# Window attention and a feed-forward net on one core: joining a pair's transposes to the next scores in one step of TensorE, with four PSUM banks for attention and a new order

## The chip, the cores and the metric

The kernel runs on one core of one Trainium2 chip. The metric is the device time of one execution in microseconds (us), taken as the median of several runs. A core has five engines that run side by side: TensorE (PE in the profile; its weight loads are a row of their own, PEld), VectorE (DVE), ScalarE (ACT), GpSimd (POOL) and SyncE (SP), which issues the DMAs. Only TensorE multiplies matrices. It writes into PSUM, eight banks of 128 partitions x 512 float32, and DVE and ACT read the banks out again.

## The reference, cut to what matters

Eight batches, eight heads, 512 local and 32 global positions, head dimension 64; then a feed-forward net on 4352 tokens of 512 features with 2048 hidden ones.

```
s_g   = scale * q_g @ k_all.T            # 32 global queries see all 544 keys
out_g = sm(s_g) @ v_all
s_ll  = where(|i - j| <= 32, scale * q_l @ k_l.T, -1e9)    # 512 local queries: a window
s_lg  = scale * q_l @ k_g.T                                # and the 32 global keys
out_l = sm(concat(s_lg, s_ll)) @ concat(v_g, v_l)
x     = attention's output, heads side by side: (4352, 512)
h     = x @ w_in;  out = (h - tanh(h)) @ w_out
```

## The kernel before, in words

**Attention.** Heads go in pairs (class `Pair`), 32 of them, four to a batch; a pair's two heads sit on the two halves of the 128 partitions. A pair has four tiles of 128 local queries, taken in two halves (`tp` 0 and 1, two tiles each). A half goes through these steps:

- *Scores* (`add_head_scores`, L588): keys of a window of 192 and the 32 globals against 128 queries, 64 rows of the array at a time. Two PSUM banks, one for each head. From the third batch on ("split" pairs, 24 of them) keys and queries are each a rounded high part and a rest, and three products are added: 12 matmuls. In the first two batches they are plain float32, which the profile shows as 8.
- *Softmax* (`Head.add_softmax`, `add_norms`): the maximum with the mask, from the banks into `prob` (DVE, L866); the exponential (ACT, L873); the inverse of the sum (DVE, L603 and L604); the scaling (POOL, L610).
- *Transposes* (`add_transposes`, L631): 16 small matmuls turn the probabilities, again 64 rows at a time, into two banks, one for each half of the rows; two copies bring them to `keys_first` (DVE or ACT, L309).
- *Product* (`add_product`, L655): the turned probabilities with the values, 64 columns of the array at a time, into one bank; then DVE and ACT write it as the high part and the rest of x (`x_hi`, `x_lo`, L309 and L666).

The global queries of a pair have steps of their own (L515 and L516 in the first two batches, L747 and L748 after), with softmax and a transpose (on TensorE in the first two batches, L555; on DVE after, L790). The first two batches also turn keys and queries on TensorE (L482).

**Feed-forward.** A batch of 512 rows makes a `Chunk` of 16 steps. *Hidden* (`add_hidden`, L936): three parts of four matmuls, 128 rows x 128 columns of the array with 512 moving columns, into one bank; tanh on ACT (L944), a subtraction on DVE (L947) that frees the bank, then the high part (`ghi`) and the rest (`glo`, POOL L953). *Out* (`add_out`, L984): three parts of four matmuls, one for each 128 rows, into four banks that are kept for the whole chunk. The weights come as 64-bit numbers and are taken apart on chip while the first batches' attention runs.

**Who decides the order.** The kernel writes nothing down by hand. Each step is given to `Order.add` with the engines that can do it, a cost, a due time, what it reads and writes and the PSUM banks that it takes (`alloc`) and gives back (`free`). `Order.run` then plays the whole program through once while the kernel is built: it picks again and again the step that can start first, the due time deciding among those that start within `TOL` of each other, and calls the steps' functions in the order of the starts. Each engine then runs its instructions in that order. The due times are offsets of the table `CFG`. TensorE's steps have a mode: "f" (the whole array, feed-forward), "r" (64 rows: scores and transposes) and "c" (64 columns: products); the player adds `SWITCH` where it changes.

**Banks.** Banks 4 to 7 are the out steps' sums. Banks 0 to 3 are for hidden steps ("h"); attention from the second batch on ("att") may use 0, 1 and 2 of them. In the first batch it may use all eight.

**Names.** `prob` has one buffer for each head and tile parity from the second batch on, so a half's softmax can't start to write before the other half's transposes have read. The split keys and queries (`kw`, `hl`, `hi`, `wraw`), the raw loads (`rawkq`) and the values have one buffer each.

Of the kernel before, what the change touches and what calls it, by code (L numbers as in the profile page):

```python
# [16 lines left out]
P = 128  # L17
# [28 lines left out]
class Op:  # L46
    __slots__ = ("eng", "fn", "due", "n", "ready", "succ", "alloc", "free", "lat", "start", "end", "args", "seq", "xfer", "rows", "ldw", "tail", "lock", "mode")


class Order:  # L50
# [14 lines left out]
    def add(self, eng, fn, due, r=(), w=(), res=(), alloc=(), free=(), lat=0.0, xfer=0.0, rows=1.0, ldw=0.107, tail=0.107, lock=False, mode="f"):  # L65
        o = Op()
# [19 lines left out]
        for k in w:  # L86
            self.writer[k] = o
            self.readers[k] = []
        self.ops.append(o)
# [17 lines left out]
    def run(self):  # L107
# [8 lines left out]
        out = []  # L116
        while left:
            best = None
            for o in ready:
# [26 lines left out]
            ready.remove(o)  # L146
            left -= 1
# [36 lines left out]
def kernel(ctx, tc, q_l, k_l, v_l, q_g, k_g, v_g, w_in, w_out, out):  # L184
# [89 lines left out]
    def bank(shape, j, dt=F32):  # L274
# [6 lines left out]
        elif len(shape) == 4:  # L281
# [4 lines left out]
    CFG = dict(a_g=0.1528, a_kg=0.2722, a_ph=0.3445, a_qs=0.5857, a_w=0.1978, a_wn=0.303, a_xg=0.0853, d_g=28.2389, d_gl=1.4069,  # L286
               d_kg=0.574, d_kq=0.0553, d_ph=0.7721, d_pl=0.4774, d_qh=0.1505, d_qs=0.7921, d_tg=914.3225, d_tp=0.5309,
               d_w=61.785, d_wl=29.9535, d_wn=2.2777, d_xg=0.8447, d_y=0.1584, gfirst=0, ho=18.3348, hs=7.7357, lag=58.6742,
               last=24.9751, o_st0=69.8962, o_st1=113.8499, o_tw0=-1431.7355, o_tw1=129.7041, one=0, p0=160.4863, pen=3.9779,
               penp=0.8319, s_g=0.3958, s_gl=0.5029, s_kq=0.6844, s_p=0.1545, s_tg=40.9569, s_w=0.5334, s_wl=0.6576,  # L290
               step=38.5209, step1=-59.4443, lag0=99.5779, hs0=26.4451, tol=0.0037, xs=0.0037, xw=2.0259, o_ld0=-383.5097,
               o_tn0=1414.0372, o_sg0=1109.3583, o_tg0=75.7936, o_s0=247.2865, o_sp0=242.3207, o_t0=1074.9507, o_tpp0=394.0123,
               o_vl0=1388.0707, o_vl1=952.0056, o_pv0=1892.5728, o_pvp0=670.2065, o_ld1=347.8113, o_pv1=573.0431,
               o_pvp1=217.9889, o_s1=-211.9116, o_sg1=-321.0909, o_sp1=169.903, o_t1=-1979.8578, o_tg1=442.9271, o_tn1=464.4544,
               o_tpp1=-937.5482, ho0=79.3549, o_tg=2112.2434, o_pv=263.2194, o_pvp=714.503, o_s=-1629.8233, o_sp=859.0595,
               o_t=-381.019, o_tpp=-111.4941, o_tn=-1300.494, o_ld=40.8961, o_lq=274.0963, o_sg=-2095.3744, o_st=-628.0791,
               o_tw=-371.5237, o_vl=-1824.1943, o_gl=170.0508, a_kw=0.0458, d_kw=0.5405, s_kw=0.8377, wdi=19.213, wdo=0.1788)
# [4 lines left out]
    order = Order({"att": (0, 1, 2), "h": (0, 1, 2, 3), "acc": (4, 5, 6, 7), None: tuple(range(8))})  # L302
# [141 lines left out]
    class Pair:  # L444
# [126 lines left out]
        def add_head_scores(self, tp):  # L571
# [3 lines left out]
            def mm(e, tags):  # L575
# [14 lines left out]
            due = self.due(self.C["o_s"] + self.C["o_sp"] * tp)  # L590
            reads = ["kw0", "kl0", "kg0", "hk0", "lq"] if split else self.key[2:]
            add(("T", 0.76 if split else 0.85), mm, due, r=reads, w=names, res=[a.p(tp) for a in self.heads],
                alloc=[(n, self.tag) for n in names], rows=0.8 if split else 1.0, tail=0.093 if split else 0.187, mode="r")
            for a in self.heads:
                a.add_softmax(tp)
            self.add_norms(tp)

# [19 lines left out]

        def add_transposes(self, tp):
            names = [(f"t{tp}{x}", self.j) for x in range(2)]
            box = {}  # L620

            def mm(e, tags):
                for x in range(2):
                    box[x] = bank([P, 2, 4, 64], tags[names[x]])
                for h, a in enumerate(self.heads):
                    for i in range(2):
                        src = a.pt(2 * tp + i)
                        for c in range(2):
                            for x in range(2):
                                r = slice(64 * x, 64 * x + 64)  # L630
                                nc.tensor.transpose(box[x][:, h, 2 * c + i], src[r, c * P:(c + 1) * P], idn[r, r])  # L631

            def store(x):
                def fn(e, _):
                    copy(e, view(keys_first[:, 0, tp], [(2 * 768, 2), (192, 4), (1, 64)], 64 * x), box[x])
                return fn

            due = self.due(self.C["o_t"] + self.C["o_tpp"] * tp)
            add(("T", 0.55), mm, due, r=[a.p(tp) for a in self.heads] + ["idr"], w=names, res=[f"h{tp}0", f"h{tp}1"], alloc=[(n, self.tag) for n in names],
                rows=0.7, ldw=0.053, tail=0.053, mode="r")  # L640
            for x in range(2):
                add(either(512, "tp", True), store(x), due + 0.5, r=[names[x]], w=[f"h{tp}{x}"], free=[(names[x], 1)])
# [264 lines left out]
    class Chunk:  # L907
# [8 lines left out]
        def add_hidden(self, s):  # L916
# [52 lines left out]
        def add_out(self, s):  # L969
# [22 lines left out]
            if last:  # L992
                for tt in range(nt):
                    g = [(tt, f, wi, gi, f - fs[0]) for f in fs for wi, gi in passes]
                    add(("T", 0.2305 * len(g)), mm(g), due + 0.1 * tt, r=[gk, lk] + wk, w=[accs[tt], ("ord", self.name)])
            else:
                for i, (wi, gi) in enumerate(passes):
                    g = [(tt, f, wi, gi, f - fs[0]) for f in fs for tt in range(nt)]
                    add(("T", 0.2305 * len(g)), mm(g), due + 0.1 * i, r=[(gk, lk)[gi]] + wk, w=accs,
# [87 lines left out]
    def attention(j):  # L1087
        p, split = pairs[j], j >= H
        if split:
            p.add_keys()  # L1090
            p.add_split_global_scores()
        else:
            p.add_turn()
            p.add_global_scores()
            if j + 1 == H // 2:
                add_first_globals(1)
            if j + 2 < H // 2:
                pairs[j + 2].add_load()
            elif H // 2 <= j + 1 < H:
                pairs[j + 1].add_load()  # L1100
        for a in p.heads:
            a.add_values()
        if split:
            for h in range(2):
                p.add_split_global_transpose(h)
        else:
            p.add_global_transpose()
        for tp in range(2):
            p.add_head_scores(tp)
            if tp and H <= j + 1 < len(pairs):  # L1110
                if (j + 1) % (H // 2) == 0:
                    add_globals(pairs[j + 1].b)
                pairs[j + 1].add_split()
            p.add_transposes(tp)
# [100 lines left out]
```

## Time and profile before

| | before |
|---|---|
| median of 3 runs | 1007.95 us (1007.91 to 1008.49) |
| the profiled execution: time, span | 1008.14 us, 1006.4 us |
| busy: PE, PEld | 985.8, 786.5 us |
| busy: DVE, ACT, POOL | 467.2, 520.6, 447.9 us |
| PE waits after 110 us | none |
| first feed-forward matmul | at 60.03 us |

All durations come from one profiled execution. Its time is 1.7 us more than its span, which runs from the first instruction to the last, and 0.19 us more than the median of the runs. The timeline lists runs of equal instructions with the start of the first, the time from there to the end of the last, and their count. Ends of matmuls are modelled and overlap; what one costs is read from start to start.

### The profile page before, as it was taken

Reading aid. Unit: us, or ns where it says so; the run is one execution under the profiler, and the core shown is the slowest. Engines: PE = TensorE matmul, PEld = TensorE weight load, DVE = VectorE, ACT = ScalarE, POOL = GpSimd, SP = SyncE. Lnnn points to the kernel's source line nnn. Section 1 sums busy time; section 2 is a strip of 40 time slices with the busy share of each in tenths; the row PEclk is TensorE's granted clock in tenths of the full one; section 3 lists DMA queues with packets and bytes.
Section 4 is the critical chain, followed back from the end, with each engine's and each line's share of the span. In section 5 each row is a group of like instructions: output and inputs, shape, how many; then the busy total and the mean of one; then the engine's idle time right before and its main releaser. Section 6 shows DMA issues by size and latency. Waiting matters only on the chain.

```text
span 1006.4 us, 18022 instructions
## 1 busy us (share of the span) xinstructions
PE 985.8 (98%) x6352; PEld 786.5 (78%) x6352; DVE 467.2 (46%) x1532; ACT 520.6 (52%) x1444; POOL 447.9 (45%) x575
## 2 busy tenths in 40 slices
PE   7799999999999999999999999999999999999997
PEld 5567777787777778877877787778787788888896
DVE  6986556644445554444544444544444442111110
ACT  6877666555545555555545454655555453322221
POOL 4676756544435454445443444344534342322221
PEclk9889999999999999999999999999999999999999
DMA  8666333321222221321212121321222200100010
GB/s 216 175 193 182 99 78 93 82 45 29 42 56 67 40 43 29 77 40 34 52 29 77 36 36 31 79 44 25 51 39 72 40 2 19 42 1 1 1 42 22
DMA packets 203130, 59.36 MB, mean 59 GB/s; under 512 B 187936, under 2 KB 196128, under 8 KB 203040
## 3 DMA queue, kind: packets, MB, share of 16 engines
q1 hardware_dynamic: 203040, 58.21, 24.4%
q8 instruction: 50, 0.82, 0.3%
q14 instruction: 40, 0.33, 0.1%
HBM read 49.27 MB, written 8.91 MB: 58 GB/s over the span
## 4 chain that ended last, share of the span: by engine, by line
PE 95%; DVE 2%; SPq 1%; ACT 1%; DMA 1%; issue 0%; DVEq 0%
PE bank L936 38%; PE bank L984 38%; PE bank L655 7%; PE bank L588 5%; PE bank L631 4%; PE bank L747 1%; PE bank L748 0%; DMA first_q<-in_moe_w_in_dram 0%; PE bank L482 0%; DVE keys_first L309 0%; SPq L466 0%; DVE st L603 0%; PE bank L515 0%; DVE prob L866 0%; DMA first_raw<-in_k_l_dram 0%
## 5 line engine op out<-in xcount | busy, mean ns | idle before, releaser
L953 POOL TENSOR_TENSOR glo<-t,ghi 128x512 fp32r<-128x512 f32 x136 | 175.9, 1293 | 358.8 <-ACT ghi L309 218.0
L947 DVE TENSOR_TENSOR t<-bank,t 128x512 f32<-128x512 f32 x136 | 94.0, 691 | 237.3 <-ACT t L944 236.7
L944 ACT ACTIVATE t<-bank 128x512 f32<-128x512 f32 x136 | 81.5, 599 | 172.5 <-PE bank L936 168.8
L610 POOL TENSOR_SCALAR prob<-prob,st 128x224 f32<-128x224 f32 x240 | 107.1, 466 | 108.2 <-DVE st L604 100.6
L984 PE MATMUL bank<-w_out_hi,glo 128*128 128x512 f32 x544 | 153.4, 396 | 0.0
L984 PE MATMUL bank<-w_out_hi,ghi 128*128 128x512 f32 x544 | 152.6, 394 | 0.0
L984 PE MATMUL bank<-w_out_lo,ghi 128*128 128x512 f32 x544 | 151.2, 392 | 0.0
L873 ACT ACTIVATE prob<-prob,st 128x224 f32<-128x224 f32 x240 | 112.8, 472 | 59.0 <-DVE st L866 58.9
L936 PE MATMUL bank<-x_lo,w_in_hi 128*128 128x512 f32 x512 | 142.0, 399 | 0.0
L936 PE MATMUL bank<-x_hi,w_in_lo 128*128 128x512 f32 x512 | 140.3, 396 | 0.0
L936 PE MATMUL bank<-x_hi,w_in_hi 128*128 128x512 f32 x512 | 138.5, 392 | 1.3 <-DVE x_hi L309 1.3
L866 DVE CUSTOM_DVE_ANT_0 prob<-bank,mask 128x224 f32<-128x224 f32 x240 | 79.8, 387 | 95.1 <-PE bank L588 93.9
L984 PEld LDWEIGHTS bank<-w_out_hi,glo 128*128 128x128 f32 x544 | 99.8, 188 | 24.1 <-issue 4.2
L984 PEld LDWEIGHTS bank<-w_out_hi,ghi 128*128 128x128 f32 x544 | 100.6, 188 | 22.9 <-issue 1.6
L984 PEld LDWEIGHTS bank<-w_out_lo,ghi 128*128 128x128 f32 x544 | 101.2, 188 | 21.6 <-issue 0.7
L309 ACT CAST ghi<-t 128x512 fp32r<-128x512 f32 x136 | 84.7, 622 | 54.7 <-DVE t L947 45.5
L936 PEld LDWEIGHTS bank<-x_hi,w_in_hi 128*128 128x128 f32 x512 | 94.4, 188 | 22.3 <-ACT keys_first L309 1.7
L936 PEld LDWEIGHTS bank<-x_hi,w_in_lo 128*128 128x128 f32 x512 | 93.7, 188 | 22.8 <-issue 4.0
L936 PEld LDWEIGHTS bank<-x_lo,w_in_hi 128*128 128x128 f32 x512 | 92.8, 188 | 22.4 <-issue 0.6
L309 ACT COPY keys_first<-bank 128x512 f32<-128x512 f32 (+2 forms) x126 | 56.6, 496 | 78.2 <-PE bank L631 77.2
L655 PE MATMUL bank<-keys_first,values 128*64 128x160 f32 (+2 forms) x1024 | 82.3, 302 | 3.8 <-DVE keys_first L309 3.3
L655 PEld LDWEIGHTS bank<-keys_first,values 128*64 128x64 f32 (+1 forms) x1024 | 64.1, 139 | 11.6 <-DVE keys_first L309 3.9
(144 smaller groups left out, 1174.7 us busy)
## 6 DMA issues: line engine op xcount, KB each, us to landing
out_dram<-wpair SPq DMA_DIRECT2D x32, 256.0 KB, 2.0
values<-in_v_l_dram SPq DMA_DIRECT2D x63, 128.0 KB, 2.3
rawkq<-in_k_l_dram SPq DMA_DIRECT2D x96, 64.0 KB, 2.3
rawkq<-in_q_l_dram SPq DMA_DIRECT2D x96, 64.0 KB, 2.2
values<-in_v_l_dram SPq DMA_DIRECT2D x63, 64.0 KB, 2.5
stage<-in_moe_w_out_dram SPq DMA_DIRECT2D x6, 512.0 KB, 4.1
first_q<-in_moe_w_in_dram SPq DMA_DIRECT2D x6, 512.0 KB, 4.2
wpair<-in_moe_w_out_dram SPq DMA_DIRECT2D x6, 512.0 KB, 4.1
```

The costliest lines, as they stand in the source:

```text
L309: (nc.scalar.copy if e == "A" else nc.vector.tensor_copy)(dst, src)
L588: nc.tensor.matmul(x[:, i, :KC], q, k, start=n == 0, stop=n == len(passes) - 1)
L610: nc.gpsimd.tensor_scalar(x, x, st[:, c:c + 1], 1.0, op0=ALU.mult, op1=ALU.mult)
L631: nc.tensor.transpose(box[x][:, h, 2 * c + i], src[r, c * P:(c + 1) * P], idn[r, r])
L655: nc.tensor.matmul(box["o"][h.e:h.e + D, o0:o0 + c1 - c0], values[:k, h.two, a, t], keys_first[:k, h.two, pair, a, c0:c1], start=i == 0, s ...
L866: nc.vector.tensor_tensor_reduce(out=self.pt(2 * tp + i)[:, :KC], in0=getattr(self, f"s_{tp}")[:, i, :KC], in1=tile_mask[2 * tp + i], scal ...
L873: nc.scalar.activation(x, x, AF.Exp, bias=col[:, c0 + i:c0 + i + 1], scale=-1.0, accum_out=col[:, 8 + c0 + i:9 + c0 + i])
L936: nc.tensor.matmul(self.h[s][:, j * n:(j + 1) * n], w[:, cc, f * P:(f + 1) * P], self.x()[xi][:, cc, :n], start=part == 0 and cc == 0 and ...
L944: nc.scalar.activation(tt_[q], self.h[s], AF.Tanh)
L947: nc.vector.tensor_sub(tt_[q], self.h.pop(s), tt_[q])
L953: eng[e].tensor_sub(gg[q][1], tt_[q], f32(gg[q][0]))
L984: nc.tensor.matmul(self.acc[tt], g[:, j * self.n + tt * P:j * self.n + (tt + 1) * P], low_out(f) if wi else high_out(f), start=s == 0 and ...
```

## The change

It does four things. (1) From the third batch on, a pair's transposes of one half and the scores that come next are one visit: `add_visit` gives the player both steps, the first holds the banks of both and waits for what both read, and the field `next` makes the player place the second right behind the first on TensorE. With half 0's transposes go the same pair's scores of half 1; with half 1's go the next pair's scores of half 0, so that the next pair's keys and queries are made before the present pair is done. (2) Attention may take four banks, 0 to 3, from the second batch on. (3) The costs that the player uses for feed-forward matmuls are a little lower, and a step that follows another on TensorE counts as ready without the 0.06 between them. (4) The whole table `CFG` is new, and so is the order of everything. The reads and writes and the number of matmuls, exponentials and DMAs stay as they are.

```diff
@@ class Order
+        o.next = None
+        if glue is not None:
+            glue.next, o.args = o, glue.args
...
+        forced = None
         while left:
             best = None
-            for o in ready:
+            for o in ready if forced is None else [forced]:
...
             ready.remove(o)
+            forced = o.next
...
-                x.ready = max(x.ready, done + (0.06 if same else self.SEM[e]))
+                x.ready = max(x.ready, done + (self.SEM[e] if not same else 0.0 if e == "T" else 0.06))
@@ the table (one line of it) and the banks
-               step=38.5209, step1=-59.4443, lag0=99.5779, hs0=26.4451, tol=0.0037, xs=0.0037, xw=2.0259, o_ld0=-383.5097,
+               step=126.079, step1=21.2806, lag0=117.1894, hs0=56.6249, tol=0.0795, xs=0.0659, xw=9.5452, o_ld0=-439.2206,
...
-    order = Order({"att": (0, 1, 2), "h": (0, 1, 2, 3), "acc": (4, 5, 6, 7), None: tuple(range(8))})
+    order = Order({"att": (0, 1, 2, 3), "h": (0, 1, 2, 3), "acc": (4, 5, 6, 7), None: tuple(range(8))})
@@ class Pair
+        def add_visit(self, due, parts):
+            own = [n for x in parts for n in x["names"]]
+            reads = [k for x in parts[1:] for k in x["r"] if k not in parts[0]["r"]]
+            last = None
+            for i, x in enumerate(parts):
+                last = add(("T", x["d"]), x["fn"], due, r=x["r"] + (reads if i == 0 else []), w=x["names"], res=x["res"],
+                           alloc=[(n, self.tag) for n in own] if i == 0 else (), rows=x["rows"], ldw=x["ldw"], tail=x["tail"],
+                           mode="r", glue=last)
...
+        def add_both(self, tp, other):
+            t = self.transposes(tp)
+            self.add_visit(self.due(self.C["o_t"] + self.C["o_tpp"] * tp), [t, other.scores(1 - tp)])
+            self.add_turned(tp, t)
+            other.add_softmaxes(1 - tp)
@@ class Chunk
-                add(("T", 0.92), mm(part), due + 0.1 * part, r=r, w=[hk],
+                add(("T", 0.907), mm(part), due + 0.1 * part, r=r, w=[hk],
@@ the program
+    def split_attention(j):
+        p, more = pairs[j], j + 1 < len(pairs)
+        if j == H:
+            p.add_keys()
+            p.add_head_scores(0)
+        p.add_split_global_scores()
+        for a in p.heads:
+            a.add_values()
+        for h in range(2):
+            p.add_split_global_transpose(h)
+        p.add_both(0, p)
+        if more:
+            next_keys(j)
+            pairs[j + 1].add_keys()
+            p.add_both(1, pairs[j + 1])
+        else:
+            p.add_transposes(1)
+        for tp in range(2):
+            p.add_product(tp)
```

What it makes of TensorE's order is seen in a stretch with split pairs. Before, on TensorE, with equal rows left out: transposes (L631, the 16 of one half), a product (L655), then feed-forward (L984 is out, L936 is hidden), and only then scores (L588), feed-forward behind them again. Banks 98 to 101 in the names are the shared banks 0 to 3.

```order
L936 MATMUL bank_101<-x_hi_998,w_in_lo 128x512 x4
L631 MATMUL bank_98<-idr,prob_95 128x64
...
L655 MATMUL bank_100<-keys_first,values 64x160 x4
L655 MATMUL bank_100<-keys_first,values 64x128 x4
L984 MATMUL bank_102<-w_out_hi,glo_73 128x512
...
L936 MATMUL bank_98<-x_hi_998,w_in_hi 128x512 x4
...
L588 MATMUL bank_99<-kw,hi_1888 128x224
...
L936 MATMUL bank_98<-x_lo_999,w_in_hi 128x512 x4
```

The changed kernel on TensorE, the second visit of a pair and the first of the next (L612 transposes, L594 scores, L689 products, L970 hidden, L1018 out):

```order
L612 MATMUL bank_98<-idr,prob_95 128x64
...
L594 MATMUL bank_101<-kw,hi_1925 128x224
...
L689 MATMUL bank_98<-keys_first,values 64x160 x4
...
L689 MATMUL bank_99<-keys_first,values 64x160 x4
...
L970 MATMUL bank_100<-x_hi_920,w_in_hi 128x512 x4
L970 MATMUL bank_100<-x_lo_921,w_in_hi 128x512 x4
L970 MATMUL bank_100<-x_hi_920,w_in_lo 128x512 x4
L1018 MATMUL bank_105<-w_out_hi,ghi_70 128x512
...
L1018 MATMUL bank_105<-w_out_lo,ghi_70 128x512
...
L612 MATMUL bank_101<-idr,prob_95 128x64
...
L594 MATMUL bank_99<-kw,hi_1925 128x224
L594 MATMUL bank_100<-kw,hi_1925 128x224
```

Transposes, scores and both products of a pair now stand together; between this visit and the next one's transposes stand one hidden step (12 matmuls) and eight out matmuls. The next visit's second score bank is the hidden step's own, bank 100.

The second place is DVE behind such a visit. Before: the maxima of a half (L866), and right behind them the inverse of the sums (L603, L604).

```order
L866 ISA prob_96,st_92<-bank_100,mask_89 128x224
...
L866 ISA prob_95,st_92<-bank_98,mask_90 128x224
...
L603 TENSOR_SCALAR st_92<-st_92 128x4
L604 RECIPROCAL st_92<-st_92 128x4
L947 TENSOR_TENSOR t_68<-bank_99,t_68 128x512
```

Now, on DVE after the visit with two products: the maxima (L900), both products' high parts and rests (L315, L700), and only then the inverse (L663, L664).

```order
L900 ISA prob_95,st_92<-bank_101,mask_90 128x224
...
L315 CAST x_hi_920<-bank_98 128x256
L315 CAST x_hi_920<-bank_100 128x256
L700 TENSOR_TENSOR x_lo_921<-bank_98,x_hi_920 128x256
L704 COPY xg<-bank_98 128x32
L700 TENSOR_TENSOR x_lo_921<-bank_100,x_hi_920 128x256
L702 TENSOR_TENSOR xg<-bank_100,xg 128x32
L663 TENSOR_SCALAR st_92<-st_92 128x4
L664 RECIPROCAL st_92<-st_92 128x4
```

The inverse has moved behind the second product's eviction. Over the whole program 109 copies have moved from ACT to DVE (on DVE 1532 instructions before, 1641 now); the `x_hi` casts went to DVE (14 before, 62 now), and the copies of transposes to ACT (94 before, 122 now).

More of the change, by code (lines that the diff above doesn't have):

```diff
@@ L46 @@
 class Op:
-    __slots__ = ("eng", "fn", "due", "n", "ready", "succ", "alloc", "free", "lat", "start", "end", "args", "seq", "xfer", "rows", "ldw", "tail", "lock", "mode")
+    __slots__ = ("eng", "fn", "due", "n", "ready", "succ", "alloc", "free", "lat", "start", "end", "args", "seq", "xfer", "rows", "ldw", "tail", "lock", "mode", "next")
 class Order:
@@ L283, in bank @@
         return t
[L286 to L290, printed above, removed]
-               step=38.5209, step1=-59.4443, lag0=99.5779, hs0=26.4451, tol=0.0037, xs=0.0037, xw=2.0259, o_ld0=-383.5097,
[L292 to L297, printed above, removed]
@@ L569, in add_global_transpose, with scores @@
                     free=[(tg, 2)])
-        def add_head_scores(self, tp):
+        def scores(self, tp):
             names = [(f"s{tp}", a.i) for a in self.heads]
@@ L588, in mm @@
                             nc.tensor.matmul(x[:, i, :KC], q, k, start=n == 0, stop=n == len(passes) - 1)
[L590 to L593, printed above, removed]
+            return dict(fn=mm, d=0.76 if split else 0.85, names=names, r=["kw0", "kl0", "kg0", "hk0", "lq"] if split else self.key[2:],
+                        res=[a.p(tp) for a in self.heads], rows=0.8 if split else 1.0, ldw=0.107, tail=0.093 if split else 0.187)
@@ new lines, in transposes, with mm @@
+        def transposes(self, tp):
+            names = [(f"t{tp}{x}", self.j) for x in range(2)]
+            box = {}
+            def mm(e, tags):
+                for x in range(2):
+                    box[x] = bank([P, 2, 4, 64], tags[names[x]])
+                for h, a in enumerate(self.heads):
+                    for i in range(2):
+                        src = a.pt(2 * tp + i)
+                        for c in range(2):
+                            for x in range(2):
+                                r = slice(64 * x, 64 * x + 64)
+                                nc.tensor.transpose(box[x][:, h, 2 * c + i], src[r, c * P:(c + 1) * P], idn[r, r])
+            return dict(fn=mm, d=0.55, names=names, r=[a.p(tp) for a in self.heads] + ["idr"], res=[f"h{tp}0", f"h{tp}1"],
+                        rows=0.7, ldw=0.053, tail=0.053, box=box)
@@ L596, in add_head_scores, with add_turned, store, fn @@
             self.add_norms(tp)
+        def add_turned(self, tp, t):
+            names, box = t["names"], t["box"]
+            def store(x):
+                def fn(e, _):
+                    copy(e, view(keys_first[:, 0, tp], [(2 * 768, 2), (192, 4), (1, 64)], 64 * x), box[x])
+                return fn
+            due = self.due(self.C["o_t"] + self.C["o_tpp"] * tp)
+            for x in range(2):
+                add(either(512, "tp", True), store(x), due + 0.5, r=[names[x]], w=[f"h{tp}{x}"], free=[(names[x], 1)])
         def add_norms(self, tp):
@@ L616, in add_norms @@
                 add(("P", 0.9), norm(a), d + 2.5, r=[vk], w=[a.p(tp)])
[L618 to L642, printed above, removed]
         def add_product(self, pair):
@@ L1132 @@
         if i % 2 == 0:
-            attention(i // 2)
+            (attention if i < 2 * H else split_attention)(i // 2)
         if i == 2 * H - 1:
```

64 lines of the change are left out of this document (39 added, 25 removed).

## The prediction

> **What bounds the kernel now.** I read the page first, then TensorE's waits, then its timeline in one stretch of split pairs. From the page:
>
> ```profile
> span 1006.4 us, 18022 instructions
> PE 985.8 (98%) x6352; PEld 786.5 (78%) x6352; DVE 467.2 (46%) x1532; ACT 520.6 (52%) x1444; POOL 447.9 (45%) x575
> PE   7799999999999999999999999999999999999997
> ```
>
> TensorE is busy in every slice but the first two and the last, the other engines half the time; the view of TensorE's waits names none after 110 us. So the time is TensorE's own stream, and a change gains only if that stream gets shorter. Busy time can't show that, since it counts modelled ends. Starts do. TensorE's timeline, where feed-forward matmuls run undisturbed, and what a scores step and a transposes step among them cost:
>
> ```profile
> 301.49 1.07 PE L936 MATMUL bank<-x_hi,w_in_hi 128*128 128x512 f32 x4
> 302.49 0.37 PE L588 MATMUL bank<-kw,hi 64*128 64x224 f32 x2
> 302.70 0.27 PE L588 MATMUL bank<-hl,hi 64*128 64x224 f32 x2
> ...
> 303.35 0.50 PE L984 MATMUL bank<-w_out_hi,ghi 128*128 128x512 f32 x1
> 303.69 0.39 PE L984 MATMUL bank<-w_out_lo,ghi 128*128 128x512 f32 x1
> 303.92 0.40 PE L984 MATMUL bank<-w_out_hi,glo 128*128 128x512 f32 x1
> 304.15 1.08 PE L936 MATMUL bank<-x_lo,w_in_hi 128*128 128x512 f32 x4
> 305.07 1.07 PE L936 MATMUL bank<-x_hi,w_in_hi 128*128 128x512 f32 x4
> ...
> 318.12 1.07 PE L984 MATMUL bank<-w_out_hi,ghi 128*128 128x512 f32 x4
> ...
> 321.75 1.07 PE L984 MATMUL bank<-w_out_hi,glo 128*128 128x512 f32 x4
> 322.75 0.71 PE L631 MATMUL bank<-idr,prob 64*128 64x64 f32 x16
> 323.39 1.20 PE L936 MATMUL bank<-x_lo,w_in_hi 128*128 128x512 f32 x4
> 324.42 1.07 PE L984 MATMUL bank<-w_out_hi,ghi 128*128 128x512 f32 x4
> ```
>
> From 318.12 to 321.75 sixteen feed-forward matmuls start: 0.2269 us each. Whatever a visit of attention costs is the time between two feed-forward starts around it, less 0.2269 for each feed-forward matmul in between. Scores alone: 301.49 to 305.07 is 3.58 with eleven, so 1.08. Transposes alone: 321.75 to 324.42 is 2.67 with eight, so 0.855. Much of that is not work: the first feed-forward matmul behind the scores stays 0.34 in front (303.35 to 303.69) instead of 0.227, and the scores start 0.09 later than the fourth matmul's 0.227 would have it. These edges are paid once a visit, so the question is how many visits there are and what a joint between two attention steps saves against two visits.
>
> **The change, part by part.**
>
> *Joints that exist already.* Transposes next to a product, scores next to a product, a product alone (in this order):
>
> ```profile
> 309.28 1.08 PE L984 MATMUL bank<-w_out_hi,ghi 128*128 128x512 f32 x4
> 310.29 1.20 PE L655 MATMUL bank<-keys_first,values 128*64 128x160 f32 x16
> 311.42 0.71 PE L631 MATMUL bank<-idr,prob 64*128 64x64 f32 x16
> 312.06 1.21 PE L984 MATMUL bank<-w_out_lo,ghi 128*128 128x512 f32 x4
> 313.11 1.09 PE L936 MATMUL bank<-x_hi,w_in_hi 128*128 128x512 f32 x4
> 314.13 0.37 PE L588 MATMUL bank<-kw,hi 64*128 64x224 f32 x2
> ...
> 314.99 1.26 PE L655 MATMUL bank<-keys_first,values 128*64 128x160 f32 x16
> 316.18 1.20 PE L984 MATMUL bank<-w_out_hi,glo 128*128 128x512 f32 x4
> 317.21 1.07 PE L936 MATMUL bank<-x_lo,w_in_hi 128*128 128x512 f32 x4
> ```
>
> ```profile
> 85.80 1.07 PE L984 MATMUL bank<-w_out_hi,ghi 128*128 128x512 f32 x4
> 86.80 1.26 PE L655 MATMUL bank<-keys_first,values 128*64 128x160 f32 x16
> 87.98 1.19 PE L936 MATMUL bank<-x_hi,w_in_hi 128*128 128x512 f32 x4
> 89.02 1.08 PE L984 MATMUL bank<-w_out_lo,ghi 128*128 128x512 f32 x4
> ```
>
> Each has eight feed-forward matmuls, 1.815. A product alone: 3.22 - 1.815 = 1.405. Product and transposes: 309.28 to 313.11, 3.83 - 1.815 = 2.015, against 1.405 + 0.855 apart: the joint saves 0.245. Scores and product: 313.11 to 317.21, 4.10 - 1.815 = 2.285, against 2.485: it saves 0.20. In these joints the shape of the array changes (64*128 to 128*64).
>
> *Joints that are new.* Transposes and scores both use 64*128. Before has no such joint in the steady part, but one in the start-up, in float32, beside the same scores alone:
>
> ```profile
> 42.27 0.42 PE L588 MATMUL bank<-first_kw,first_q 64*128 64x224 f32 x1
> 42.29 0.22 PE L631 MATMUL bank<-idr,t 64*128 64x64 f32 x1
> 42.35 0.97 PE L588 MATMUL bank<-first_kw,first_q 64*128 64x224 f32 x7
> ```
>
> ```profile
> 94.18 1.03 PE L588 MATMUL bank<-first_kw,first_q 64*128 64x224 f32 x8
> ```
>
> The scores start even before the last transpose (42.27 against 42.29): no edge at all. From the last transpose's start to the end of the scores pass 42.35 + 0.97 - 42.29 = 1.03, what the scores take alone. So a joint visit is: 0.09 to enter, 0.71 - 0.22 = 0.49 from the first to the last transpose, and the scores' 1.08 less their own 0.09, 0.99; together 1.57, where the two apart cost 1.935. The joint saves 0.365, I take 0.37. At the low end it saves no more than a joint with a change of shape, 0.20. At the high end the scores' first step shrinks too: it takes 0.21 (302.49 to 302.70) where the other five, to 303.35 and with the edge behind them, take 0.13 each at most, so I estimate 0.1 more, 0.47.
>
> [...] The row at 42.27 shows no such shrinking, so I keep 0.37.
>
> Two products in a row have one shape too. By the same reading the second adds its own length from first to last start, about 1.26 - 0.30 = 0.96, and a step of 0.06, 1.02 in place of 1.405: it saves 0.38 (ends 0.20 and 0.45).
>
> *How many.* Counted in the order of both kernels, after the first feed-forward matmul:
>
> - Before: 44 joints of transposes and a product, 7 of scores and a product, 2 of global scores and a product (taken as 0.24). Saved: 44 x 0.245 + 7 x 0.20 + 2 x 0.24 = 10.8 + 1.4 + 0.5 = 12.7.
> - Now: 50 of transposes and scores, 23 of two products, 24 of scores and a product, 3 of transposes and a product, 6 others (0.24). Saved: 50 x 0.37 + 23 x 0.38 + 24 x 0.20 + 3 x 0.245 + 6 x 0.24 = 18.5 + 8.7 + 4.8 + 0.7 + 1.4 = 34.1.
>
> The stretches of feed-forward matmuls between visits fall from 149 to 95, as they should with 53 more joints. The difference is 34.1 - 12.7 = 21.4 us, all on the path, since TensorE never waits there. The number of matmuls is the same, so nothing else on TensorE changes.
>
> *The start.* Before the first feed-forward matmul stand the same TensorE steps in both orders, though in another sequence, and VectorE sets the pace there:
>
> ```profile
> 25.00:50.00 25.00, 18.33 (x206) 13.94 (x208) 24.17 (x88) 22.42 (x72) 16.69 (x27) 0.89 0.67 176
> 60.03 0.96 PE L936 MATMUL bank<-x_hi,w_in_hi 128*128 128x512 f32 x3
> ```
>
> The columns are PE, PEld, DVE, ACT, POOL: DVE is busy 24.17 of 25. In the order DVE has 194 instructions up to the first batch's last `x_lo`, now 196, of nearly the same kinds. I take 0, with 2 us either way.
>
> *What is hidden.* The 109 copies that went from ACT to DVE lie beside TensorE on an engine that is 46% busy. The loads are the same, and a pair's keys and values, though single-buffered, have the time between two visits to arrive. The lower costs and the 0.06 change only the played order. Four banks for attention cost nothing as long as the hidden step gives its bank back in time (third rival).
>
> **The sum.** 1008.14 - 21.4 = 986.7 for the profiled execution, which lay 0.19 above the median: 986.5.
>
> **The rivals.** Their prices rest on these groups of the page (the number before the last bar is the mean ns):
>
> ```profile
> L947 DVE TENSOR_TENSOR t<-bank,t 128x512 f32<-128x512 f32 x136 | 94.0, 691 | 237.3 <-ACT t L944 236.7
> L944 ACT ACTIVATE t<-bank 128x512 f32<-128x512 f32 x136 | 81.5, 599 | 172.5 <-PE bank L936 168.8
> L610 POOL TENSOR_SCALAR prob<-prob,st 128x224 f32<-128x224 f32 x240 | 107.1, 466 | 108.2 <-DVE st L604 100.6
> L873 ACT ACTIVATE prob<-prob,st 128x224 f32<-128x224 f32 x240 | 112.8, 472 | 59.0 <-DVE st L866 58.9
> L866 DVE CUSTOM_DVE_ANT_0 prob<-bank,mask 128x224 f32<-128x224 f32 x240 | 79.8, 387 | 95.1 <-PE bank L588 93.9
> ```
>
> 1. *The softmax comes late.* From the visit with two products to the next transposes TensorE has about 2.0 of products and 20 feed-forward matmuls, 4.5: some 6.5 us. The chain in that time is a maximum 0.39, four exponentials 1.9, four scalings 1.9, 4.2 with nothing between; but DVE's inverse now stands behind the second product's eviction, which can't start before that product ends, 2 us in. For it: the order. Against: 2 us of slack. If the transposes come 0.4 late at 23 visits, 9 us are lost: 996.
> 2. *The joint of transposes and scores isn't special* and saves 0.20: 50 x 0.17 = 8.5 less, 995. Against it stands the row at 42.27.
> 3. *Slower: the fourth bank.* A joint visit takes all four shared banks, and the last hidden step before it holds one until tanh (0.60) and the subtraction (0.69) are done. In the order eight out matmuls (1.8) and the transposes (0.5) stand between that step and the scores that want its bank: 2.3 against 1.3. It decides where tanh falls behind a half's exponentials on ACT, 1.9 more: then the scores are about 0.9 late. Beyond 21.4 / 47 = 0.46 a visit the change is slower; at about 0.55 for all 47 visits it is 26 lost, 1012. [...]
> 4. *It does nothing*: stalls of 0.4 to 0.5 us at each visit eat just what the joints give, 1006 to 1010.
>
> **How the numbers follow.** Forecast 0.76, softmax 0.10, joint not special 0.06, fourth bank 0.05, nothing 0.03. The likeliest is 986.5. The low end, 981, is the forecast with the hidden first load; the start's 2 us lie inside. The upper end, 996, takes in both rivals that lose 9. Outside it are the last two, and the tails. A measurement of this kernel tells about 0.2%, 2 us. Faster: 0.76 + 0.10 + 0.06 = 0.92; same 0.03; slower 0.05.
>
> **What would show it.** Right: no wait of TensorE after the start; transposes and scores as neighbours with about 1.57 for the visit by the same counting of starts; 0.34 in front of the second feed-forward matmul about 54 times fewer; a first feed-forward matmul near 60. Wrong: waits of L612 for POOL's scaling (first rival), an edge of 0.2 between L612 and L594 (second), waits of L594 for DVE's L981 (third), a first feed-forward matmul off by more than 2 us (the start).

## The result, and the profile after

The median went from 1007.93 us (1007.72 to 1008.49) to 985.99 us (985.44 to 987.84), a ratio of 0.9784 with a 95% interval of 0.9770 to 0.9799: 22 us faster, where 21.4 were forecast. The profiled execution took 985.88 us. From its page:

```profile
span 984.0 us, 18093 instructions
PE 961.6 (98%) x6352; PEld 785.5 (80%) x6352; DVE 525.0 (53%) x1641; ACT 489.3 (50%) x1335; POOL 445.2 (45%) x575
PE   7789999999999999999999999999999999999997
```

TensorE is as full as it was, with the same 6352 instructions; its stream got shorter. The span lost 22.4. The start gave 0.8 of it, as the first feed-forward matmul shows, which stood at 60.03:

```profile
59.25 0.96 PE L970 MATMUL bank<-x_hi,w_in_hi 128*128 128x512 f32 x3
```

The rest lies in the visits. Both kernels start the same 3360 feed-forward matmuls, so the time between the first and the last of these starts tells what the visits cost in sum. It was 940.8 us before (60.03 to 1000.80) and is 919.2 now (59.25 to 978.49): 21.5 less. TensorE's timeline over one visit of transposes and scores, which is the joint that is new (start, time to the end of the last, then line and form):

```profile
301.22 0.39 PE L1018 MATMUL bank<-w_out_hi,glo 128*128 128x512 f32 x1
301.54 0.71 PE L612 MATMUL bank<-idr,prob 64*128 64x64 f32 x16
302.06 0.35 PE L594 MATMUL bank<-kw,hi 64*128 64x224 f32 x2
302.25 0.28 PE L594 MATMUL bank<-hl,hi 64*128 64x224 f32 x2
...
302.69 0.28 PE L594 MATMUL bank<-kw,wraw 64*128 64x224 f32 x2
302.90 0.50 PE L1018 MATMUL bank<-w_out_hi,ghi 128*128 128x512 f32 x1
303.23 0.40 PE L1018 MATMUL bank<-w_out_lo,ghi 128*128 128x512 f32 x1
303.47 0.39 PE L1018 MATMUL bank<-w_out_hi,glo 128*128 128x512 f32 x1
303.70 1.08 PE L970 MATMUL bank<-x_hi,w_in_hi 128*128 128x512 f32 x4
```

From 301.22 to 303.70 are 2.48 us with four feed-forward matmuls: the visit costs 1.57, as forecast. The scores start 0.52 behind the first transpose (302.06 to 301.54), 0.03 more than the 0.49 that the prediction took from the first transpose to the last: there is no edge between the two. The 0.32 in front of the visit and the 0.33 in front of the second feed-forward matmul are paid once now.

The other visit of a pair, with both products behind the scores:

```profile
319.71 1.07 PE L1018 MATMUL bank<-w_out_hi,glo 128*128 128x512 f32 x4
320.71 0.71 PE L612 MATMUL bank<-idr,prob 64*128 64x64 f32 x16
321.23 0.35 PE L594 MATMUL bank<-kw,hi 64*128 64x224 f32 x2
...
322.10 2.24 PE L689 MATMUL bank<-keys_first,values 128*64 128x160 f32 x32
324.27 1.20 PE L970 MATMUL bank<-x_hi,w_in_hi 128*128 128x512 f32 x4
325.30 1.07 PE L970 MATMUL bank<-x_lo,w_in_hi 128*128 128x512 f32 x4
```

That is 5.59 less 1.815, 3.775 for four steps. By the prediction's prices the four apart cost 0.855 + 1.08 + 2 x 1.405 = 4.745, and its three joints save 0.37 + 0.20 + 0.38 = 0.95, which leaves 3.795. Over all visits the trace has 24 of the first kind, with a median of 1.58, and 23 of the second, with a median of 3.78.

How near the waits came is read from the other engines in front of the next pair's first visit. The rows of ACT, DVE, POOL and TensorE:

```profile
325.87 0.18 DVE L664 RECIPROCAL st<-st 128x4 f32<-128x4 f32 x1
326.25 1.73 POOL L670 TENSOR_SCALAR prob<-prob,st 128x224 f32<-128x224 f32 x4 [4.01 <-DVE st L664]
327.38 0.60 ACT L978 ACTIVATE t<-bank 128x512 f32<-128x512 f32 x1 [2.48 <-PE bank L970]
328.01 0.69 DVE L981 TENSOR_TENSOR t<-bank,t 128x512 f32<-128x512 f32 x1 [0.58 <-ACT t L978]
329.02 0.71 PE L612 MATMUL bank<-idr,prob 64*128 64x64 f32 x16
329.55 0.35 PE L594 MATMUL bank<-kw,hi 64*128 64x224 f32 x2
```

The scalings end at 327.98, 1.04 before the transposes that read them. The slack is the same at 16 of the 47 visits and larger at the others; before the change it was mostly 2.4 to 2.6. The subtraction ends at 328.70, 0.85 before the scores, one of which writes the bank that it frees. Both rivals' paths are there, and both have about a microsecond to spare. The view of TensorE's waits names none from 70 us to the end.

### The profile page after: what moved, and what is told of

Its sections match the earlier page's. It is cut to its first block, busy times and chain, and to the rows that moved or that the text cites. A ratio compares the mean times of both kernels' runs of the same rounds, so it can differ in the third digit from the quotient of the medians.

```text
span 984.0 us, 18093 instructions
## 1 busy us (share of the span) xinstructions
PE 961.6 (98%) x6352; PEld 785.5 (80%) x6352; DVE 525.0 (53%) x1641; ACT 489.3 (50%) x1335; POOL 445.2 (45%) x575
## 4 chain that ended last, share of the span: by engine, by line
PE 94%; DVE 2%; DMA 1%; POOL 1%; issue 1%; ACT 0%; SPq 0%; DVEq 0%; POOLq 0%
PE bank L1018 39%; PE bank L970 38%; PE bank L689 7%; PE bank L594 4%; PE bank L612 4%; PE bank L781 1%; DMA wpair<-in_moe_w_out_dram 1%; PE bank L488 1%; PE bank L782 1%; PE bank L521 0%; DMA stage<-in_moe_w_in_dram 0%; POOL prob L670 0%; DVE keys_first L315 0%; DMA first_raw<-in_k_l_dram 0%; DVE prob L900 0%
## 5 line engine op out<-in xcount | busy, mean ns | idle before, releaser
L1018 PE MATMUL bank<-w_out_hi,glo 128*128 128x512 f32 x544 | 152.8, 395 | 0.0
L1018 PE MATMUL bank<-w_out_hi,ghi 128*128 128x512 f32 x544 | 152.3, 394 | 0.0
L1018 PE MATMUL bank<-w_out_lo,ghi 128*128 128x512 f32 x544 | 150.3, 390 | 0.0
L970 PE MATMUL bank<-x_hi,w_in_hi 128*128 128x512 f32 x512 | 140.4, 395 | 1.5 <-DVE x_hi L315 1.5
L970 PE MATMUL bank<-x_lo,w_in_hi 128*128 128x512 f32 x512 | 137.4, 390 | 0.0
L970 PE MATMUL bank<-x_hi,w_in_lo 128*128 128x512 f32 x512 | 137.4, 390 | 0.0
L900 DVE CUSTOM_DVE_ANT_0 prob<-bank,mask 128x224 f32<-128x224 f32 x240 | 79.9, 387 | 84.9 <-PE bank L594 79.7
L1018 PEld LDWEIGHTS bank<-w_out_hi,ghi 128*128 128x128 f32 x544 | 100.9, 188 | 23.4 <-issue 2.0
L1018 PEld LDWEIGHTS bank<-w_out_lo,ghi 128*128 128x128 f32 x544 | 101.8, 188 | 21.5 <-issue 0.5
L1018 PEld LDWEIGHTS bank<-w_out_hi,glo 128*128 128x128 f32 x544 | 99.3, 188 | 22.0 <-issue 0.7
L970 PEld LDWEIGHTS bank<-x_hi,w_in_hi 128*128 128x128 f32 x512 | 94.1, 188 | 25.8 <-issue 4.5
L970 PEld LDWEIGHTS bank<-x_hi,w_in_lo 128*128 128x128 f32 x512 | 95.7, 188 | 20.2 <-issue 0.2
L970 PEld LDWEIGHTS bank<-x_lo,w_in_hi 128*128 128x128 f32 x512 | 95.6, 188 | 20.2
L315 ACT CAST ghi<-t 128x512 fp32r<-128x512 f32 x129 | 80.0, 620 | 60.9 <-PE bank L1018 56.1
L315 ACT COPY keys_first<-bank 128x512 f32<-128x512 f32 (+2 forms) x154 | 71.4, 515 | 64.6 <-PE bank L612 60.3
L689 PE MATMUL bank<-keys_first,values 128*64 128x160 f32 (+2 forms) x1024 | 76.1, 295 | 5.8 <-DVE keys_first L315 4.7
L689 PEld LDWEIGHTS bank<-keys_first,values 128*64 128x64 f32 (+1 forms) x1024 | 63.5, 137 | 12.5 <-DVE keys_first L315 3.6
```

What stands on the lines that cost most here:

```text
L315: (nc.scalar.copy if e == "A" else nc.vector.tensor_copy)(dst, src)
L689: nc.tensor.matmul(box["o"][h.e:h.e + D, o0:o0 + c1 - c0], values[:k, h.two, a, t], keys_first[:k, h.two, pair, a, c0:c1], start=i == 0, s ...
L900: nc.vector.tensor_tensor_reduce(out=self.pt(2 * tp + i)[:, :KC], in0=getattr(self, f"s_{tp}")[:, i, :KC], in1=tile_mask[2 * tp + i], scal ...
L970: nc.tensor.matmul(self.h[s][:, j * n:(j + 1) * n], w[:, cc, f * P:(f + 1) * P], self.x()[xi][:, cc, :n], start=part == 0 and cc == 0 and ...
L1018: nc.tensor.matmul(self.acc[tt], g[:, j * self.n + tt * P:j * self.n + (tt + 1) * P], low_out(f) if wi else high_out(f), start=s == 0 and ...
```

## The experiments

The theory is that of the prediction: the gain is the number of visits, each joint saves its price, and nothing waits. Against it stood: the joint of transposes and scores is not special; four banks or the new table bring the gain by themselves; the softmax or the fourth bank has no room. Times are medians of four or more executions, if nothing else is said; the time of before beside them lay at 1007.98 to 1008.46.

**1. One new joint undone: feed-forward matmuls between transposes and scores.** In the order that the player has made, the four matmuls in front of each such visit go between its two steps, at 47 visits.

```diff
+        for v in [v for v in out if v[2].next is not None]:
+            i = out.index(v)
+            k = max(n for n in range(i) if out[n][3] == "T")
...
+            out.insert(i, out.pop(k))
```

> The changed kernel's own order, but in each of the 47 joint visits of the split pairs the four feed-forward matmuls that stood just ahead of the transposes now stand between the transposes and the scores. Theory of edges: each joint of transposes and scores loses the 0.37 us that it saved (1.58 us joined in the changed kernel's trace, 0.867 + 1.088 apart), 47 x 0.373 = 17.5: 1003.5 us, and no new wait of TensorE. Rival, the joint is no better than one with a change of shape (0.20 to 0.245): 47 x 0.22 = 10, 996 us. Rival, the gain is the new table and start, not the joints: 986 us.

It took 1001.99 us (1001.90 to 1005.08), 0.9944 of before (0.9929 to 0.9958): 16.0 more than the changed kernel, 0.34 for each visit; from the first feed-forward start to the last it is 16.5 longer, 0.35 each. The same place in its timeline:

```profile
302.98 0.39 PE L1023 MATMUL bank<-w_out_hi,glo 128*128 128x512 f32 x1
303.30 0.71 PE L617 MATMUL bank<-idr,prob 64*128 64x64 f32 x16
303.94 0.50 PE L1023 MATMUL bank<-w_out_hi,ghi 128*128 128x512 f32 x1
...
304.83 0.37 PE L599 MATMUL bank<-kw,hi 64*128 64x224 f32 x2
305.04 0.28 PE L599 MATMUL bank<-hl,hi 64*128 64x224 f32 x2
...
306.03 0.40 PE L1023 MATMUL bank<-w_out_lo,ghi 128*128 128x512 f32 x1
306.27 0.40 PE L1023 MATMUL bank<-w_out_hi,glo 128*128 128x512 f32 x1
306.51 1.09 PE L975 MATMUL bank<-x_hi,w_in_hi 128*128 128x512 f32 x4
```

From 302.98 to 306.51 are 3.53 with seven feed-forward matmuls (1.59): 1.94, against 1.57 joined. Here the joint is worth 0.37, and the view of TensorE's waits still names none after 70 us. The rival by which it isn't special is out, and most of the gain is in this one place.

**2. The other new joint undone: the two products of a pair apart.** The second product goes behind the next four feed-forward matmuls, at 23 visits (the lines that mark the products of the split pairs are left out).

```diff
+        t = [v for v in out if v[3] == "T"]
+        for x, y, z in zip(t, t[1:], t[2:]):
+            if x[2].kind == y[2].kind == "product" and z[2].mode == "f":
+                i = out.index(y)
+                out.insert(out.index(z), out.pop(i))
...
```

> The changed kernel's own order, but in the 23 visits with two products the second product moves behind the next four feed-forward matmuls. Theory of edges: 23 x 0.38 = 8.7 lost, 994.7 us. If the joint of two products is worth no more than one with a change of shape, 23 x 0.20 = 4.6: 990.6 us. If joints do not matter: 986 us. The inverse of the next softmax stands behind the second product's eviction, so it comes some 0.9 us later against 1.04 us of slack in the changed kernel's trace: should TensorE wait for POOL's scaling here, the slack was smaller than read.

It took 994.86 us (994.59 to 995.50), 0.9866 (0.9852 to 0.9881): 8.9 more, 0.386 for each visit, where 0.38 was the forecast. Part of that is a later start: from the first feed-forward start to the last it is 8.4 longer, 0.36 each. One such visit in its timeline:

```profile
321.59 1.07 PE L1024 MATMUL bank<-w_out_hi,glo 128*128 128x512 f32 x4
...
326.23 1.26 PE L694 MATMUL bank<-keys_first,values 128*64 128x160 f32 x16
...
328.45 1.08 PE L976 MATMUL bank<-x_hi,w_in_lo 128*128 128x512 f32 x4
```

From 321.59 to 328.45 are 6.86 with twelve feed-forward matmuls (2.72): 4.14, against 3.78 with the products joined. This run also tries the first rival, since the second product's eviction comes later and the inverse of the sums behind it. POOL's scalings and the transposes that wait for them:

```profile
329.40 1.74 POOL L675 TENSOR_SCALAR prob<-prob,st 128x224 f32<-128x224 f32 x4 [5.29 <-DVE st L669]
...
331.28 0.71 PE L617 MATMUL bank<-idr,prob 64*128 64x64 f32 x16
```

The scalings end at 331.14, and the slack has shrunk from 1.04 to 0.14, at 16 places of the trace alike, with no loss. So the rival's chain is real, and it had a microsecond of room.

**3. The visit undone as a rule of the player, the rest kept.** Transposes and scores are given to the player as two steps; banks, table, costs and the order of the program stay.

```diff
-            self.add_visit(self.due(self.C["o_t"] + self.C["o_tpp"] * tp), [t, other.scores(1 - tp)])
+            self.add_visit(self.due(self.C["o_t"] + self.C["o_tpp"] * tp), [t])
...
-            other.add_softmaxes(1 - tp)
+            other.add_head_scores(1 - tp)
```

> The changed kernel with its table, banks and costs, but transposes and scores are two steps again, each placed by the player on its own. The order it makes has 99 stretches of feed-forward matmuls (95 with the glue, 149 before); after the start 27 joints of transposes and scores, 26 of transposes and a product, 43 of scores and a product, none of two products. Theory of edges, by the sum's prices: saved 27 x 0.37 + 26 x 0.245 + 43 x 0.20 + 6 x 0.24 = 26.4 against 34.1 with the glue: 7.7 lost, 993.7 us, more if a visit waits inside. Rival, the undivided step itself is the gain: near 1005 us.

It took 996.06 us (995.89 to 996.41), 0.9879 (0.9862 to 0.9895): the rule is worth 10.1 of the 22 us. The player left to itself puts some of the pairs together all the same. From the first feed-forward start to the last it is 10.2 longer, where 7.7 were expected. Of the rest 1.7 is a wait at five visits, which its timeline shows between the first score step and the second:

```profile
302.94 0.71 PE L594 MATMUL bank<-kw,hi 64*128 64x224 f32 x2
303.29 0.48 PE L594 MATMUL bank<-hl,hi 64*128 64x224 f32 x2
```

The two stand 0.35 apart, in place of 0.19, and such a visit costs 1.94, where the others of its sort cost 1.60. The waits' view doesn't list it.

**4 to 6. The other parts, put into the kernel before.** Four banks and the new table together, the table alone, the banks alone (one line of the table stands for all).

```diff
...
-               step=38.5209, step1=-59.4443, lag0=99.5779, hs0=26.4451, tol=0.0037, xs=0.0037, xw=2.0259, o_ld0=-383.5097,
+               step=126.079, step1=21.2806, lag0=117.1894, hs0=56.6249, tol=0.0795, xs=0.0659, xw=9.5452, o_ld0=-439.2206,
...
-    order = Order({"att": (0, 1, 2), "h": (0, 1, 2, 3), "acc": (4, 5, 6, 7), None: tuple(range(8))})
+    order = Order({"att": (0, 1, 2, 3), "h": (0, 1, 2, 3), "acc": (4, 5, 6, 7), None: tuple(range(8))})
```

> The kernel before, its program and costs, with only the four banks and the new table. Its order has 109 stretches of feed-forward matmuls and, after the start, 27 joints of transposes and scores, 25 of transposes and a product, 35 of scores and a product, 5 others. Theory of edges: saved 10.0 + 6.1 + 7.0 + 1.2 = 24.3 against 12.7 before: 11.6 gained, 996.3 us, if no wait appears. Rival, the joint step is what gains: 1006 to 1008 us. Rival, table and banks are the whole gain: 986 us.

> The kernel before with only the new table; attention keeps three banks. Its order has 142 stretches of feed-forward matmuls (149 before) and, after the start, 3 joints of transposes and scores, 17 of transposes and a product, 34 of scores and a product, 6 others. Theory of edges: saved 1.1 + 4.2 + 6.8 + 1.4 = 13.5 against 12.7: 0.8 gained, 1007 us, or more than that where a wait appears. Rival, the table itself is worth something: under 1003 us.

> The kernel before with only the four banks and its old table. Its order has 147 stretches and 8 joints of transposes and scores, 5 of two products, 29 of scores and a product, 6 of transposes and a product, 1 other. Theory of edges: saved 3.0 + 1.9 + 5.8 + 1.5 + 0.2 = 12.4 against 12.7: 1008 us, more with a wait. Rival, the fourth bank alone is worth something: under 1003 us.

Together they took 1002.41 us (1002.31 to 1002.50), 0.9940 (0.9926 to 0.9955). The table alone took 1021.34 us (1019.92 to 1023.07), 1.0118 (1.0099 to 1.0138), and the banks alone 1016.69 us (1015.56 to 1019.47), 1.0076 (1.0054 to 1.0097). All three expectations missed, by 6, 14 and 9 us, on the same side and for the same reason: they counted joints and took it that nothing waits. TensorE's timeline with the table alone, where the split pairs begin:

```profile
189.51 0.27 PE L632 MATMUL bank<-idr,prob 64*128 64x64 f32 x1
191.67 0.65 PE L632 MATMUL bank<-idr,prob 64*128 64x64 f32 x14 [1.89 <-DVE st L758]
...
193.07 0.40 PE L589 MATMUL bank<-kw,hi 64*128 64x224 f32 x1 [0.59 <-ACT keys_first L310]
...
193.28 0.61 PE L589 MATMUL bank<-kw,wraw 64*128 64x224 f32 x2
193.48 0.62 PE L589 MATMUL bank<-kw,hi 64*128 64x224 f32 x2
```

In the middle of a half's transposes TensorE waits 1.89 for DVE's maximum of the global scores (L758). The transposes don't read it, but it gives back the two banks of the global scores. Then the scores wait 0.59 for a copy that gives back a bank of the transposes. So both are waits for banks, of which attention has three here. The score steps that follow stand 0.20 apart where they stand 0.11 otherwise: they run at about half pace. The same stretch in the view of stretches (busy time of PE, PEld, DVE, ACT and POOL, then the granted clock):

```profile
150.00:200.00 50.00, 43.94 (x313) 31.27 (x312) 30.57 (x117) 26.58 (x84) 22.46 (x36) 0.90 0.41 95
```

The granted clock is 0.90 of full over these 50 us (0.991 over the whole trace, 0.990 over that of before). By an estimate from this, 50 x 0.10, at most 5 of the 14.8 us by which the table alone is longer between the first and the last feed-forward start are the clock's in this stretch; the rest is the waits themselves and the order. With the banks alone waits of up to 1.35 lie at 174 to 213 us. With both they are small; the view of TensorE's waits has

```profile
PE bank L589 <- ACT keys_first L310: 1.0, 2, 0.5
PE bank L632 <- POOL prob L611: 0.8, 3, 0.5
PE bank L937 <- DVE x_hi L310: 0.4, 1, 0.4
```

and the starts show another 4 us inside visits, five visits of them with the 0.35 of experiment 3. So the parts don't add up. From before, the table costs 13.1 and the banks cost 8.4, and both together gain 6.0; with the visit as a rule, and the order of the program that goes with it, the gain is 22. Between both together (1002.41) and experiment 3 (996.06) lie the lower costs, the 0.06 and the order of the program: they bring 6.3, and no run takes these three apart. Neither the table nor the banks bring the gain by themselves.

**7 and 8. Tanh two and three times** (the cut shows two). This delays the bank that the visit's second score waits for; the same value is computed again.

```diff
-                nc.scalar.activation(tt_[q], self.h[s], AF.Tanh)
+                for _ in range(2):
+                    nc.scalar.activation(tt_[q], self.h[s], AF.Tanh)
```

> The changed kernel's order with each hidden step's tanh done twice into the same place, so that the shared bank comes back 0.60 us later. In the changed kernel's trace the scores of 33 of the 47 joint visits start 0.84 us after the subtraction that frees the fourth bank, and 5 more 1.07 us after. Theory of the fourth bank with this slack: 0.60 fits into 0.84, 986 to 987 us. Rival, the fourth bank is already at its limit: 33 x 0.4 or more, over 999 us.

> The same with tanh three times, 1.20 us later. Theory of the fourth bank with 0.84 us of slack: the scores wait 0.36 us at 33 visits and 0.13 at 5, 12.5 us, some 998 us, and the waits stand at the scores behind the transposes. Rival, the bank never decides: 986 to 988 us. A wait of the transposes for POOL's scaling instead would say that ACT's queue delays the exponentials.

Twice took 986.97 us (986.45 to 988.87), 0.9783 (0.9766 to 0.9801): 0.60 more fits into the 0.85, and 0.21 is left at 33 visits. Three times took 1009.67 us (1008.20 to 1010.54), 1.0007 (0.9998 to 1.0016): the whole gain is gone. The place in its timeline:

```profile
327.94 0.60 ACT L979 ACTIVATE t<-bank 128x512 f32<-128x512 f32 x1
328.32 0.71 PE L612 MATMUL bank<-idr,prob 64*128 64x64 f32 x16
328.56 0.69 DVE L982 TENSOR_TENSOR t<-bank,t 128x512 f32<-128x512 f32 x1 [2.02 <-ACT t L979]
328.84 0.84 PE L594 MATMUL bank<-kw,hi 64*128 64x224 f32 x2
329.31 0.48 PE L594 MATMUL bank<-hl,hi 64*128 64x224 f32 x2
```

The subtraction ends at 329.25, the second score of the visit (the other head's, into the freed bank) can start only then, and the next row stands 0.47 behind the first score, in place of 0.19. The trace has this 0.47 at 33 visits and 0.25 at five, the very visits that were expected to wait. But a visit with 0.47 costs 0.48 more than the same visit of the changed kernel, and one with 0.25 costs 0.27 more, where 0.36 and 0.13 had been counted: 33 x 0.48 + 5 x 0.27 = 17.2 of the 22.9 by which the time from the first feed-forward start to the last rose. Another 4.6 are lost before 185 us, in the first two batches. The expectation, 998, priced the visits too low and had nothing for those batches. The scalings still end at least 0.8 before the transposes at every joint visit, so it isn't the softmax. The waits' view of TensorE names 1.3 us of all this after 100 us; the chain that ended last shows it, by engine and by line:

```profile
PE 79%; ACT 10%; DVE 6%; issue 1%; DMA 1%; POOL 1%; SPq 1%; ACTq 0%; POOLq 0%; DVEq 0%
```

The changed kernel's chain has 94% on PE, 2% on DVE and nothing on ACT. So the third rival is real, with its place and its price, and decides once tanh and the subtraction come more than about 0.8 us later.

**9. The old table with the new program.** A single execution beside one of before at 1007.98.

```diff
...
-               step=126.079, step1=21.2806, lag0=117.1894, hs0=56.6249, tol=0.0795, xs=0.0659, xw=9.5452, o_ld0=-439.2206,
+               step=38.5209, step1=-59.4443, lag0=99.5779, hs0=26.4451, tol=0.0037, xs=0.0037, xw=2.0259, o_ld0=-383.5097,
...
```

> The changed kernel's program, glue, banks and costs with the old table. Its order has only 55 stretches of feed-forward matmuls (95 with the new table): 50 joints of transposes and scores, 31 of scores and a product, 6 of two products, 16 of transposes and a product; but in five batches several visits stand in a row with no feed-forward matmul between a half's scores and its transposes. Counting joints alone: about 5 us faster than the changed kernel, 981 us. Theory of the softmax chain (maximum 0.4, exponentials 1.9, scalings 1.9 and the hand-overs, 5.5 us in the traces from scores to the last scaling): about four such places in each of five batches wait some 4 us each, and the clock drops there: 20 x 4 = 80 us lost, 1060 us.

It took 1164.54 us: the direction was right, the loss more than twice what was expected. It has the fewest stretches of feed-forward matmuls of all the kernels, 55, so the most joints, and is the slowest. Six visits of 43 to 47 us, one for each batch of split pairs, hold most of the batch's attention with no feed-forward matmul in between. The beginning of one, and the page's row of the granted clock:

```profile
427.26 0.71 PE L611 MATMUL bank<-idr,prob 64*128 64x64 f32 x15 [1.28 <-DVE xg L701]
428.93 0.37 PE L593 MATMUL bank<-kw,hi 64*128 64x224 f32 x2 [0.96 <-DVE st L790]
...
430.47 3.80 PE L688 MATMUL bank<-keys_first,values 128*64 128x160 f32 x32 [0.61 <-ACT keys_first L314]
436.31 0.28 PE L611 MATMUL bank<-idr,prob 64*128 64x64 f32 x2 [2.04 <-POOL prob L669]
...
438.27 0.42 PE L593 MATMUL bank<-hl,hi 64*128 64x224 f32 x2
438.48 0.42 PE L593 MATMUL bank<-kw,wraw 64*128 64x224 f32 x2
```

```profile
PEclk8899999999589995999869997699967999589999
```

The scores' softmax now has nothing to hide behind: TensorE waits 2.04 for the scaling. It waits 1.28, 0.96 and 0.61 ahead of that, 2.85 of the 4.49 us from 425.98 (1.28 before the transposes at 427.26) to 430.47. The 32 product matmuls that start then take 3.80, where they took 2.24, and behind the wait of 2.04 the score steps stand 0.21 apart, where they stand 0.11 in the changed kernel. The view of stretches has a granted clock of 0.91 from 396 to 442 us, though the feed-forward matmuls up to 423 run at the full pace of 0.227:

```profile
396.00:442.00 46.00, 40.88 (x248) 33.26 (x247) 14.39 (x50) 17.30 (x49) 10.74 (x12) 0.91 0.15 44
```

In the page's row the slice from 436 to 465 us has 5 tenths. At the changed kernel's prices such a visit (five steps of transposes and scores, seven products, three global scores) would be 5 x 1.58 + 7 x 1.10 + 3 x 0.58 = 17.3; at 45.1 on average it loses 28, and six of them 167 of the 178 by which the time from the first feed-forward start to the last is longer. The mean granted clock is 0.904 over the 1162.8 us of this trace and 0.995 over the 984.0 of the changed kernel's, so by an estimate from these at most 112 less 5, 107 of the 178, are the clock's. The pace agrees with a halved clock: behind an earlier visit two feed-forward starts stand 0.43 apart (329.58 to 330.43), 0.227 otherwise. TensorE was not idle for long at a time: the clock fell here behind short waits that lie close together, none of them longer than 2.1 at this place.

## Why the prediction was right, point by point

- **What bounds the kernel** held: TensorE's stream. Waits of the kind that experiments 3, 4 and 8 show are absent from the changed kernel's steady part, read from starts: at 47 of 47 split visits the first score stands 0.03 behind the last transpose, and the second step 0.19 behind the first.
- **The joint of transposes and scores**: 0.37 taken, 0.34 to 0.37 measured (experiment 1).
- **Two products**: 0.38 taken, 0.36 to 0.386 measured (experiment 2).
- **The sum**: 21.4 forecast, 21.5 in the visits. The start, taken as 0 with 2 either way, gave 0.8; together they are the span's 22.4 to within 0.1.
- **The hidden first load**, the low end, was an estimate of 0.1 for each joint, and no run shows it. What the runs show is 0.02: the first score step of a joint visit takes 0.19 (302.06 to 302.25), that of scores alone 0.21 (304.83 to 305.04 in experiment 1), the later ones 0.11. The rows of the weight loads show the same: in the joint visit the first scores' load starts 0.03 ahead of its matmul (302.03 to 302.06), the next one 0.11 ahead (302.14 to 302.25). Why the first one starts so late no run here tells.
- **The softmax**: the mechanism was right, its slack was taken too large, 2 us where 1.04 was left. The step that was mis-sized is the inverse behind the second product's eviction: the products' row ends at 324.34, but DVE's reciprocal starts at 325.87, behind a cast, two rests and two small copies that come only then (some 1.4 us in all), and to which the prediction had given no time. Experiment 2 took away 0.9 of the slack, and nothing was lost: it didn't decide, but it had less room than the text said.
- **The fourth bank**: 2.3 against 1.3 was about 1.0 of slack, 0.85 was measured, and experiment 8 shows the loss that was described. The case that was to bring it, tanh behind a half's exponentials, doesn't occur: no split visit has less than 0.84. The point from which the change is slower, 0.46 lost a visit, was nearly met: with 0.37 a visit on average, and 4.6 in the first two batches, the gain was gone.
- **What would show it**: "no wait of TensorE" was too weak a sign. In experiment 8 that view is nearly as empty as in the changed kernel, with some 23 us lost. The starts were the sign to trust.
- **What was not foreseen**: that the table and the banks each lose alone, and bring the whole gain only together with the visit. The prediction priced the joints of the order as it came out and didn't need the parts; an engineer who had tried the banks or the table alone would have seen a loss and dropped them.

No run here is faster than the changed kernel. One visit for a whole pair, and the same visits in the second batch, were not tried.

## What to carry to other kernels

Where one engine's stream is the bound and it is full already, price what switching between kinds of work costs, from start to start, and count the switches: steps with the same shape of array, put side by side, saved most here (0.34 to 0.386 a joint, against 0.20 and 0.245 where the shape changes). Then show for each join that its inputs and banks arrive in time, since a join also takes away the work that hid a wait, and more joins in another order can lose eight times what these gained (178 us against 22). An order that was tuned for one program is not to be judged in another.

## What the runs showed of the hardware

- A visit can lose 0.48 us (experiment 8) with nothing in the waits' view, because the ends of the matmuls ahead are modelled and reach over most of the wait. The first score matmul claims 0.35 from 328.84, to 329.19, and the second starts at 329.31: of the 0.47 between the two starts only 0.12 is idle by these rows, and the view lists none of it.
- After a visit the feed-forward pace is not back at once. Behind the 0.33 of the second matmul the next stand 0.24 apart (303.23, 303.47) where the steady pace is 0.227; this is part of what a visit costs.
- Short waits close together were enough to bring the clock down: in experiment 9 the pace fell behind 4.49 us in which TensorE waited 2.85, with no wait over 1.28, and the page's row goes down to 5 tenths. What follows then takes up to 1.9 times as long (0.43 against 0.227 between two feed-forward starts, 0.21 against 0.11 between two score steps). By the granted clocks at most 5 of the table's 14.8 us and 107 of the old table's 178 are this, an estimate; the rest is the waits themselves and the order. The two were not measured apart.
